# Block products for the first half of the tokens, a shared ring for weight chunks, early K rows and PSUM chains in a gated attention-MLP kernel

## The chip, the cores and the metric

The kernel runs on one core of a Trainium2 chip. The metric is the device time of one execution in microseconds (us). TensorE (PE, with its weight loads as PEld) multiplies; VectorE (DVE), ScalarE (ACT) and GpSimd (POOL) do the rest; SyncE (SP) issues most transfers. Each engine works through its own instructions strictly in the order in which the program gives them, and waits for others by semaphores.

## The reference

```python
x = A_x                                            # 1 x 2048 x 576, fp32
g = sigmoid((x * gate_w).sum(-1, keepdims=True))
a = A_ref(x, A_wqkv, A_wo)     # linear attention, 32 heads of 18, phi(t) = elu(t) + 1 + 1e-6
b = (gelu(x @ w_gate) * (x @ w_up)) @ w_down       # 576 -> 4608 -> 576
return g * a + (1 - g) * b
```

Everything is fp32. The kernel multiplies with TensorE's fp32r type and splits each operand into a high part (rounded to fp32r) and a low part (the rest): three matmuls, high by high, high by low and low by high, stand for one. Copying a tile into an fp32r tile on ScalarE makes the high part; one subtraction makes the low part.

## The kernel before, in words

Part one (to about 280 us) computes keys, values and queries, the attention state, and the gated attention result `g * a`, which goes to DRAM as `ga_d`, one piece for each of the 16 tiles of 128 tokens. The first loop over token tiles (`for t in range(2, NST)`) multiplies the keys and values; beside it, `Early` already prepares the weights of the first MLP chunk: it fetches them in pieces, forms four differences on GpSimd, the high part on ScalarE and the low part on GpSimd, and stores them to DRAM (`wp_d`).

Part two is the MLP. The tokens are taken in two pairs of 512-token blocks ("the first pair", "the second pair"), the 4608 hidden units in 18 chunks of 256 (`NF2`), so there are 36 chunks `n`, two loops of 18 in one. A chunk's gate and its up matrix are both computed as a 2 x 2 block product by seven products instead of eight (Strassen-Winograd): `product(k, m, ps, start)` issues seven matmuls of 128 x 512 for product k of matrix m (0 gate, 1 up) with operands `xo` (sums of token blocks, made ahead) and `W[m]` (sums of weight blocks). A step is one product and what follows on VectorE and ScalarE. Gate's steps end in a GELU into `es[0..3]`; up's steps multiply `es` by the up result and split the result into `hs[i]`, high and low.

The down projection of a chunk is issued during the next chunk, between the steps. For the first pair it is plain: `down(n, t)` is 12 matmuls of 128 x 288 for each of eight token tiles, and VectorE adds the result, times 1 − g, to an accumulator. For the second pair (all but its last chunk) it is by seven block products as well: `unit(n, k, q)` is six matmuls for half of product k, and VectorE adds the result to one of seven sums; three more operands (`hx`) and one in `hs` are sums of `es` blocks, made on GpSimd (`h_sums`). After the last chunk the seven sums are combined on GpSimd (`combine`), and the last chunk's plain down is added with the gates.

In the first pair the weights of each chunk are made as they are needed and stored for the second: SP fetches the raw block (`w_fetch`), GpSimd forms four differences (`w_sums`), ScalarE the high and GpSimd the low parts (`w_split`), SP stores the 2.2 MB tile to `wp_d`. In the second pair they are loaded from there (`w_load`). The sums of the second pair's tokens are also made during the first pair, in six pieces, each spread over two chunks (`sums_ahead`): fetched and summed in one, split and stored in the next.

PSUM has four single banks for the products (`bank()`) and two pairs of banks for the down projection (`pair()`). A new user of a buffer waits until the last reader of the old one is through. The order of the work is written out by hand: `next_down` puts units or down tiles between the steps, and each engine's queue follows the order of the program text.

Of the kernel before, what the change touches and what calls it, by code (L numbers as in the profile page):

```python
# [8 lines left out]
F32 = mybir.dt.float32  # L9
# [7 lines left out]
NB, BS = 4, 512  # L17
# [15 lines left out]
SEQUENCE = (1, 6, 2, 7, 5, 4, 3)  # L33
# [6 lines left out]
def tile_gated_mix(ctx, tc, xt, xs, wkv, wq, wo, wgu, wdn, cst, out):  # L40
# [134 lines left out]
    def kv_post(t, c, ps, part):  # L175
# [81 lines left out]

    class Early:


        def __init__(self, k):
            self.m, self.kt = divmod(k, 3)
            r, v = w_raw(), qw[k % 2].rearrange("p a c -> p (a c)")

            def part(a, c, n):
                return a[:, c * 128:(c + n) * 128].rearrange("p (i c) -> p i c", i=n)

            self.raw, self.sums, self.hi, self.lo = part(r, 0, 4), part(r, 4, 4), part(v, 0, 7), part(v, 7, 7)
            nc.sync.dma_start(self.raw, wgu[0, self.m, :, :, self.kt])

        def make(self):
            b12, b11, b21, b22 = (self.raw[:, i] for i in range(4))
            t1, t2, t3, t4 = (self.sums[:, i] for i in range(4))
            for o, a, b in ((t1, b12, b11), (t2, b22, t1), (t3, b22, b12), (t4, t2, b21)):
                nc.gpsimd.tensor_tensor(o, a, b, OP.subtract)
            for i, src in ((slice(0, 3), self.raw[:, 1:4]), (slice(3, 7), self.sums)):
                nc.scalar.activation(self.hi[:, i], src, AF.Copy)
                if self.kt < 2:
                    nc.gpsimd.tensor_tensor(self.lo[:, i], src, f32(self.hi[:, i]), OP.subtract)
                else:  # L280
                    nc.gpsimd.tensor_tensor(self.hi[64:96, i], src[64:96], f32(self.hi[64:96, i]), OP.subtract)

        def store(self):
            nc.sync.dma_start(wp_d[0][self.m][:, :, self.kt], f32(self.hi))
            if self.kt < 2:
                nc.sync.dma_start(wp_d[0][self.m][:, :, 3 + self.kt], f32(self.lo))

    early = []
    x_next(1)
    for t in range(2, NST):  # L290
# [26 lines left out]
    mixing.banks(3)  # L317
    denp = mixing.stack.enter_context(tc.tile_pool(name="denp", bufs=1, space=PSUM, reuse_waits="tile"))
# [197 lines left out]
    def mixed(b, t):  # L516
# [3 lines left out]
        for g in range(NG):  # L520
            R = GR[g]
            for a, wl in ((0, 0), (0, 1), (1, 0)):
                for i in range(2):
# [6 lines left out]
                             scale=gate[:, 0, st:st + 1])  # L530
# [564 lines left out]
```

## Time and profile before

| | us |
|---|---|
| median of 3 runs | 1556.26 (1552.9 to 1557.09) |
| span of the profiled execution | 1554.6 |
| PE busy | 1535.8 (99%) |
| DVE busy | 989.5 (64%) |
| POOL busy | 851.2 (55%) |
| ACT busy | 548.6 (35%) |
| gate and up products, PE (L690, two groups) | 433.7 + 435.8 |
| plain down, PE (L852, four groups) | 250.6 + 12.7 + 1.8 + 1.7 |
| units, PE (L876, two groups) | 123.0 + 93.0 |

The page gives no device time of its own for the profiled execution beside the span. In rows that group instructions, the columns are line, engine, operation, output <- inputs, shapes, count, then busy time in us, mean ns of one, and the idle time of the engine ahead of them with what ended it. In rows in order of time, they are start (us), length (us), engine, line, operation; the square bracket is the engine's idle time before the row and what ended it. Matmuls overlap their successors, so the distance between two starts, not the length, is what a matmul costs.

### The profile page before, as it was taken

The numbers are of one execution on the slowest core, as the hardware profiler recorded it, in microseconds if no ns is written. First come the engines' busy times: TensorE is split into PE (matmuls) and PEld (weight loads), VectorE is DVE, ScalarE is ACT, GpSimd is POOL, SyncE is SP. The second block draws the span as 40 slices with busy tenths as digits, with TensorE's granted clock in tenths as the row PEclk, the third lists the DMA queues.
The fourth block names the chain that finished last, engine by engine and source line by source line (L and its number), as shares of the span: only waits on it lengthen the run. The fifth ranks groups of instructions, "written<-read, shape, count | busy, mean of one in ns | idle before, by whom it ended". The sixth has DMA issues, their size and how long they took to land.

```text
span 1554.6 us, 21238 instructions
## 1 busy us (share of the span) xinstructions
PE 1535.8 (99%) x8447; PEld 1358.3 (87%) x8447; DVE 989.5 (64%) x1342; ACT 548.6 (35%) x848; POOL 851.2 (55%) x693
## 2 busy tenths in 40 slices
PE   8999999999999999999999999999999999999997
PEld 8999788888888888888888888888888888888886
DVE  6443767366655555565655556777777767777777
ACT  6544554333433333333333322223232223222221
POOL 1410112276777768686666646556666555666663
PEclk9999999999999999999999999999999999999999
DMA  5611434765556565565545575433443443344333
GB/s 202 194 56 32 154 126 170 254 254 188 204 203 235 218 230 202 188 242 186 215 177 194 202 312 184 180 142 134 175 167 134 148 179 134 141 186 150 134 149 107
DMA packets 53883, 275.26 MB, mean 177 GB/s; under 512 B 4368, under 2 KB 23464, under 8 KB 43160
## 3 DMA queue, kind: packets, MB, share of 16 engines
q1 hardware_dynamic: 49464, 257.26, 44.5%
q10 hardware_dynamic: 2592, 9.31, 1.6%
q0 software_dynamic: 1728, 7.34, 1.2%
q8 instruction: 66, 1.08, 0.3%
q14 instruction: 33, 0.27, 0.1%
HBM read 172.41 MB, written 101.47 MB: 176 GB/s over the span
## 4 chain that ended last, share of the span: by engine, by line
PE 91%; DVE 4%; DMA 2%; issue 1%; ACT 1%; POOL 1%; SPq 0%; ACTq 0%; DVEq 0%; POOLq 0%
PE bank L690 50%; PE pair L852 15%; PE pair L876 12%; PE bank L168 7%; PE bank L333 3%; PE pair L524 2%; PE pair L219 1%; DVE h L733 1%; DMA xc<-xs 1%; DMA wg<-wp_d 1%; POOL xo L476 1%; DVE e L727 0%; DVE sums L904 0%; PE pair L168 0%; PE den L428 0%
## 5 line engine op out<-in xcount | busy, mean ns | idle before, releaser
L690 PE MATMUL bank<-xo,wu 128*128 128x512 f32 x1764 | 435.8, 394 | 5.7 <-DVE p L790 5.7
L690 PE MATMUL bank<-xo,wg 128*128 128x512 f32 x1764 | 433.7, 393 | 0.2 <-DMA wg<-wp_d 0.2
L690 PEld LDWEIGHTS bank<-xo,wu 128*128 128x128 f32 x1764 | 323.4, 188 | 66.7 <-DVE p L790 6.6
L690 PEld LDWEIGHTS bank<-xo,wg 128*128 128x128 f32 x1764 | 324.8, 188 | 64.7 <-DMA wg<-wp_d 0.6
L852 PEld LDWEIGHTS pair<-wd,h 128*128 128x128 f32 x1716 | 243.6, 189 | 13.8 <-DVE wd L67 0.7
L852 PE MATMUL pair<-wd,h 128*128 128x288 f32 x1716 | 250.6, 294 | 0.7 <-DVE wd L67 0.5
L730 ACT ACTIVATE h<-e 128x512 fp32r<-128x512 f32 x127 | 80.4, 633 | 376.3 <-DVE e L727 349.6
L859 DVE SCALAR_TENSOR_TENSOR acc<-pair,gate,acc 128x576 f32<-128x576 f32 x143 | 116.6, 816 | 131.1 <-PE pair L852 131.1
L881 DVE TENSOR_TENSOR sums<-pair,sums 128x576 f32<-128x576 f32 x224 | 167.7, 754 | 34.3 <-PE pair L876 26.5
L733 DVE TENSOR_TENSOR h<-e,h 128x512 fp32r<-128x512 f32 x127 | 131.4, 1035 | 44.8 <-ACT h L730 44.7
L760 ACT ACTIVATE e<-e 128x512 f32<-128x512 f32 x108 | 68.1, 631 | 226.1 <-DVE e L816 93.4
L680 POOL TENSOR_TENSOR wdb<-draw,wdb 128x432 fp32r<-128x432 f32 x34 | 38.4, 1153 | 195.9 <-ACT wdb L678 195.9
L876 PEld LDWEIGHTS pair<-wdb,h 128*128 128x128 f32 x816 | 117.9, 189 | 8.3 <-DVE sums L881 0.6
L876 PE MATMUL pair<-wdb,h 128*128 128x288 f32 x816 | 123.0, 296 | 0.1
L168 PE MATMUL bank<-kvw,xo 128*128 128x378 f32 (+5 forms) x560 | 106.9, 345 | 5.4 <-ACT kvw L66 5.2
L168 PEld LDWEIGHTS bank<-kvw,xo 128*128 128x128 f32 (+1 forms) x560 | 97.0, 192 | 9.9 <-ACT kvw L66 5.6
L618 POOL TENSOR_TENSOR wu<-wuraw,wu 128x768 fp32r<-128x768 f32 x18 | 36.5, 2028 | 119.6 <-ACT wu L617 119.6
L876 PEld LDWEIGHTS pair<-wdb,hx 128*128 128x128 f32 x612 | 89.0, 189 | 6.2 <-DVE sums L881 0.6
L876 PE MATMUL pair<-wdb,hx 128*128 128x288 f32 x612 | 93.0, 296 | 0.1
L765 ACT ACTIVATE p<-bank 128x512 f32<-128x512 f32 x72 | 43.0, 598 | 122.0 <-PE bank L690 121.6
L770 DVE TENSOR_TENSOR u<-bank,p 128x512 f32<-128x512 f32 x72 | 49.4, 686 | 45.0 <-PE bank L690 39.9
L727 DVE TENSOR_TENSOR e<-u,e 128x512 f32<-128x512 f32 x72 | 69.4, 965 | 2.5
(171 smaller groups left out, 2079.2 us busy)
## 6 DMA issues: line engine op xcount, KB each, us to landing
wp_d<-wg SPq DMA_DIRECT2D x17, 2240.0 KB, 6.7
wp_d<-wu SPq DMA_DIRECT2D x17, 2240.0 KB, 8.2
wg<-wp_d SPq DMA_DIRECT2D x17, 2240.0 KB, 8.7
wu<-wp_d SPq DMA_DIRECT2D x17, 2240.0 KB, 8.4
draw<-wdn SPq DMA_DIRECT2D x36, 576.0 KB, 9.4
wgraw<-wgu SPq DMA_DIRECT2D x18, 768.0 KB, 4.4
wuraw<-wgu SPq DMA_DIRECT2D x18, 768.0 KB, 4.5
xo<-xop_d SPq DMA_DIRECT2D x7, 1280.0 KB, 8.1
```

Source lines behind the costliest of these rows:

```text
L168: nc.tensor.matmul(out_t[:, :n], xa, kvw[i][:rows, r, lo:lo + n], start=(k == 0), stop=(k == 13))
L333: nc.tensor.matmul(ps[:R], qw[i][:rows, rw, GO[g]:GO[g] + R], xa, start=(k == 0), stop=(k == 13))
L690: nc.tensor.matmul(ps, w_, x_, start=start and i == 0, stop=i == 6, skip_group_check=not start)
L727: nc.vector.tensor_tensor(es[i], v, es[i], OP.mult)
L730: nc.scalar.activation(hs[i][:, 0], es[i], AF.Copy)
L733: nc.vector.tensor_tensor(hs[i][:, 1], es[i], f32(hs[i][:, 0]), OP.subtract)
L760: nc.scalar.activation(es[i], es[i], AF.Gelu_apprx_tanh)
L770: nc.vector.tensor_tensor(u2, b, p1, OP.add)
L852: nc.tensor.matmul(y[i], h[:, a, c], wd[:, (1 - i, 2 + i)[f], wl], start=(k == 0), stop=(k == 5))
L859: nc.vector.scalar_tensor_tensor(o, v, gate[:, 1, st:st + 1], o, op0=OP.mult, op1=OP.add)
L876: nc.tensor.matmul(y[:, j, :288], h[:, hl, c], wd[:, b, wl], start=(i == 0), stop=(i == 2))
L881: nc.vector.tensor_tensor(o, y[:, :, :288], o, OP.add)
```

## The change

Four things are done. (1) The first pair's down projection also goes by units (17 of its 18 chunks), with the same `sums`, `hx` and `combine`; in the first pair the sums of h, their low parts and the low part of `wd` are made on VectorE, in the second on GpSimd. (2) Weight chunks come in halves through one ring of three tiles of 128 x 1152 (`Half`), shared by gate and up chunks, down chunks, the token pieces (now 12, each fetched and finished in one chunk) and the `ga_d` tiles. (3) The last 64 of the 576 K rows (`tail`, 32 rows in each half) of all chunks are prepared in the first loop over token tiles by `Early`, now 13 jobs instead of six, and come by six small transfers a chunk (`w_tail`). (4) Gate and up products are chained in PSUM: products 1, 6, 5, 3 accumulate in one bank and 7, 4 in another, and ScalarE copies what stands there after products 1, 6 and 5. The order of the products changes from 1, 6, 2, 7, 5, 4, 3 to 1, 7, 6, 2, 5, 3, 4.

Core of the diff (new lines, cut):

```diff
-SEQUENCE = (1, 6, 2, 7, 5, 4, 3)
+SEQUENCE = (1, 7, 6, 2, 5, 3, 4)
...
+    def block_sums(raw8, eng, c=slice(None)):
+        b12, b11, b21, b22, t1, t2, t3, t4 = (raw8[:, i, c] for i in range(8))
+        for o, a, b in ((t1, b12, b11), (t2, b22, t1), (t3, b22, b12), (t4, b21, t2)):
+            eng.tensor_tensor(o, a, b, OP.subtract)
...
+    JOBS = [("tail", 0)] + [("main", m, kt) for m in range(2) for kt in range(2)] + [("tail", i) for i in range(1, NF2 // 2)]
...
+        for _ in range(2):
+            if len(early) < len(JOBS):
+                early.append(Early(len(early), JOBS[len(early)]))
                 early[-1].make()
+                if len(early) > 1:
+                    early[-2].store()
...
+    def w_tail(n, m, queue=None):
+        q = slice((2 * m + n % 2) * 32, (2 * m + n % 2 + 1) * 32)
+        hi, lo = wt_d[n // 2]
+        for r, src in enumerate((hi, hi, lo)):
+            (queue or nc.sync).dma_start(f32(W[m][32 * r:32 * r + 32, :, 4]), src[q])
...
+    def d_split(parts, eng, plain=False):
+        for h in parts:
+            dst, src = (wd[:, :4], h.raw8[:, :4]) if plain else (wd, h.raw8[:, 1:])
+            nc.scalar.activation(dst[:, :, 0, h.c], src, AF.Copy)
+        for h in parts:
+            dst, src = (wd[:, :4], h.raw8[:, :4]) if plain else (wd, h.raw8[:, 1:])
+            eng.tensor_tensor(dst[:, :, 1, h.c], src, f32(dst[:, :, 0, h.c]), OP.subtract)
...
+    def w_make(h):
+        w = W[h.m]
+        block_sums(h.raw8, nc.gpsimd)
+        nc.scalar.activation(w[:, :, h.kt], h.raw8[:, 1:], AF.Copy)
+        nc.gpsimd.tensor_tensor(w[:, :, 2 + h.kt], h.raw8[:, 1:], f32(w[:, :, h.kt]), OP.subtract)
...
+    def x_make(h):
+        hi, lo = h.hi.bitcast(F32R), h.raw.bitcast(F32R)
+        sum_blocks(h.raw, nc.gpsimd)
+        nc.scalar.activation(hi, h.raw, AF.Copy)
+        if h.kt < 2:
+            nc.gpsimd.tensor_tensor(lo, h.raw, h.hi, OP.subtract)
+            nc.gpsimd.dma_start(xop_d[:, S2:S1 + 1, 3 + h.kt, h.c], h.raw)
...
+        nc.gpsimd.dma_start(xop_d[:, S2:S1 + 1, h.kt, h.c], h.hi)
...
+    def up_steps(plain, sum_eng, low_eng):
...
+        def s6():
+            product(6, 1, ps["a"], False)
+            nc.scalar.activation(u2, ps["a"], AF.Copy)
+        def s2():
+            c = bank()
+            product(2, 1, c, True)
+            nc.vector.tensor_tensor(c, c, p1, OP.add)
+            up(0, c)
+        def s5():
+            product(5, 1, ps["a"], False)
+            nc.scalar.activation(u3, ps["a"], AF.Copy)
+            high(hs[0], es[0])
+            nc.vector.tensor_tensor(u3, ps["b"], u3, OP.add)
+            up(3, u3)
+            low(hs[0], es[0])
+        def s3():
+            product(3, 1, ps["a"], False)
+            high(hs[3], es[3])
+            up(1, ps["a"])
+            high(hs[1], es[1])
+            low(hs[3], es[3])
+        def s4():
+            product(4, 1, ps["b"], False)
+            nc.vector.tensor_tensor(ps["b"], ps["b"], u2, OP.add)
+            up(2, ps["b"])
+            low(hs[1], es[1])
...
+            def first():
+                h_sum(3, 2, 3, OP.add)
+                h_sum(2, 0, 2, OP.subtract)
+                h_sum(0, 3, 0, OP.subtract)
+                h_sum(1, 1, 0, OP.subtract)
+                high(hb[S1], es[3])
+                high(hb[S3], es[2])
+            def second():
+                high(hb[S2], es[0])
+                high(hb[S4], es[1])
+                for a, i in ((S2, 0), (S3, 2), (S1, 3), (S4, 1)):
+                    low(hb[a], es[i], low_eng)
+            late.extend([first, second])
...
+        sum_eng, low_eng, d_eng = (nc.vector, nc.vector, nc.vector) if p == 0 else (nc.gpsimd, nc.gpsimd, nc.gpsimd)
...
+        gate_down = (0, 0, 0, 1, 1, 1, 1) if seam else (0, 0, 2, 3, 3, 2, 2) if final else (0, 0, 2, 2, 2, 2, 2)
+        for i, step in enumerate(gate_steps() if n else first_steps):
...
+            if late and i in (0, 1):
+                late.pop(0)()
+            next_down(gate_down[i])
+            if p == 0 and n:
+                if i == 0:
+                    w_tail(n, 1)
+                if i in (2, 3):
+                    w_make(ups.pop(0))
+                if i == 4:
+                    nc.sync.dma_start(wp_d[q][1], f32(W[1]))
+                    if 2 <= n < 14:
+                        xr_.append(x_fetch(n - 2))
+                if i == 5 and xr_:
+                    x_make(xr_.pop())
...
+            if i == 6:
+                if p == 0 and n + 1 < NF2:
+                    gates = w_fetch(n + 1, 0)
...
+        up_down = (0, 1, 1, 0, 2, 0, 0) if not final else (0, 0, 0, 0, 2, 0, 0)
+        for i, step in enumerate(up_steps(final, sum_eng, low_eng)):
             step()
+            next_down(up_down[i])
+            if p == 0 and n + 1 < NF2:
+                if i == 0:
+                    w_tail(n + 1, 0)
+                if i in (0, 1):
+                    w_make(gates[i])
+                if i == 2:
+                    ds = d_fetch(n)
+                    nc.sync.dma_start(wp_d[n + 1][0], f32(W[0]))
+                if i == 4:
+                    ups = w_fetch(n + 1, 1)
...
+            if not final and i == 3:
+                d_sums(ds)
+            if i == 5:
+                d_split(ds, d_eng, final)
```

`w_fetch`, `d_fetch` and `x_fetch` each take ring tiles and issue one SP transfer a tile (256 KB for weights and tokens, 288 KB for down). `combine` is called between the steps of the last chunk of both pairs.

What the engines' queues hold at three places. In the rows, `e`, `h` and `hx` are the tiles of `es`, `hs` and `hx`, and numbers tell tiles of one kind apart. First, VectorE at the turn from one chunk of the first pair to the next, before:

```order
L816 TENSOR_TENSOR u_2552<-bank,u_2552 128x512
L727 TENSOR_TENSOR e_2913<-u_2552,e_2913 128x512
L733 TENSOR_TENSOR h_2918<-e_2914,h_2918 128x512
L733 TENSOR_TENSOR h_2917<-e_2913,h_2917 128x512
L67 TENSOR_TENSOR wd<-draw,wd 128x4x288
L770 TENSOR_TENSOR u_2552<-bank,p_2551 128x512
L785 TENSOR_TENSOR u_2553<-bank,u_2552 128x512
L859 SCALAR_TENSOR_TENSOR acc_2927<-pair,gate,acc_2927 128x576
```

and now (L690 is wd's low part, L837, L799 and L751 belong to up's last product, L846 are the sums of h):

```order
L690 TENSOR_TENSOR wd<-ring,wd 128x7x144 x2
L837 TENSOR_TENSOR bank<-bank,u_2636 128x512
L799 TENSOR_TENSOR e_3001<-bank,e_3001 128x512
L751 TENSOR_TENSOR h_3004<-e_3000,h_3004 128x512
L846 TENSOR_TENSOR e_3002<-e_3001,e_3002 128x512
L846 TENSOR_TENSOR e_3001<-e_2638,e_3001 128x512
L846 TENSOR_TENSOR e_2638<-e_3002,e_2638 128x512
L846 TENSOR_TENSOR e_3000<-e_3000,e_2638 128x512
L751 TENSOR_TENSOR hx_3008<-e_2638,hx_3008 128x512
L751 TENSOR_TENSOR h_3005<-e_3001,h_3005 128x512
L751 TENSOR_TENSOR hx_3007<-e_3002,hx_3007 128x512
L751 TENSOR_TENSOR hx_3009<-e_3000,hx_3009 128x512
```

The first sums out of PSUM (L906) stand directly behind the last of these. Second, SP's queue in a chunk of the first pair, before (`xu` is the token piece):

```order
L660 DMA draw<-wdn 128x1152
L606 DMA wuraw<-wgu 128x1536
L622 DMA wp_d_1_108<-wu 128x4480
L700 DMA xu<-xs 128x4x256
L606 DMA wgraw<-wgu 128x1536
L622 DMA wp_d_0_109<-wg 128x4480
```

and now:

```order
L990 DMA wp_d_1_124<-wu 128x4480
L711 DMA ring<-xs 128x4x128
L697 DMA ring<-wgu 128x512 x2
L619 DMA wg<-wt_d_0_99 32x7x128 x2
L619 DMA wg<-wt_d_1_100 32x7x128
L674 DMA ring<-wdn 128x4x144 x2
L1023 DMA wp_d_0_125<-wg 128x4480
```

The gate chunks used to be fetched a chunk ahead, behind the token piece as now; they are now fetched for the next half of the work. Third, ScalarE around the start of the up products in the first pair, before (L705 splits a token piece, L617 the weights, L765 copies p1):

```order
L705 ACTIVATE xuh<-xu 128x1024
L776 ACTIVATE e_2554<-bank 128x512
L760 ACTIVATE e_2915<-e_2915 128x512
L760 ACTIVATE e_2914<-e_2914 128x512
L760 ACTIVATE e_2913<-e_2913 128x512
L765 ACTIVATE p_2551<-bank 128x512
L617 ACTIVATE wg<-wgraw 128x3x384
L617 ACTIVATE wg<-tsum 128x4x384
```

and now (L717 splits a token piece, L704 the weights, L804 and L812 copy p1 and u2 out of PSUM):

```order
L757 ACTIVATE e_2638<-e_2638 128x512
L757 ACTIVATE e_3002<-e_3002 128x512
L757 ACTIVATE e_3000<-bank 128x512
L717 ACTIVATE ring<-ring 128x512
L757 ACTIVATE e_3001<-e_3001 128x512
L804 ACTIVATE p_2635<-bank 128x512
L704 ACTIVATE wg<-ring 128x7x128 x2
L812 ACTIVATE u_2636<-bank 128x512
```

A copy that TensorE waits for now stands behind the two weight halves, and the token piece's split stands between the GELUs of the chunk that fetched it.

More of the change, by code (lines that the diff above doesn't have):

```diff
@@ L271, in make @@
-        def make(self):
[L272 to L281, printed above, removed]
@@ L283, in store @@
-        def store(self):
-            nc.sync.dma_start(wp_d[0][self.m][:, :, self.kt], f32(self.hi))
-            if self.kt < 2:
-                nc.sync.dma_start(wp_d[0][self.m][:, :, 3 + self.kt], f32(self.lo))
+            self.raw8 = r[:, :1024].rearrange("p (i c) -> p i c", i=8)
+            self.hi, self.lo = (v[:, a * 896:(a + 1) * 896].rearrange("p (i c) -> p i c", i=7) for a in range(2))
+            self.job = job
+            kind, *which = job
+            src = wgt[which[0]] if kind == "tail" else wgu[0, which[0], which[1]]
@@ L316, in tile_gated_mix @@
     mixing = Scope()
-    mixing.banks(3)
-    denp = mixing.stack.enter_context(tc.tile_pool(name="denp", bufs=1, space=PSUM, reuse_waits="tile"))
+    mixps = Scope()
+    mixps.banks(3)
+    denp = mixps.stack.enter_context(tc.tile_pool(name="denp", bufs=1, space=PSUM, reuse_waits="tile"))
     rp = mixing.pool("rp", bufs=3)
@@ L632, in tile_gated_mix @@
     scaled(0, 0)
-    nc.scalar.dma_start(f32(W[0]), wp_d[0][0])
+    first_load(0)
     mixed(3, 3)
@@ L676, in d_split, with __init__, as8 @@
-    def d_split():
-        for i, src in ((slice(0, 3), draw[:, 1:4]), (slice(3, 7), dsum)):
-            nc.scalar.activation(wd[:, i, 0], src, AF.Copy)
-            for c in (slice(0, 144), slice(144, 288)):
-                nc.gpsimd.tensor_tensor(wd[:, i, 1, c], src[:, :, c], f32(wd[:, i, 0, c]), OP.subtract)
+    class Half:
+        def __init__(self):
+            self.t = ring.tile([128, 1152], F32, name="ring")
+        def as8(self, c):
+            return self.t[:, :8 * c].rearrange("p (i c) -> p i c", i=8)
@@ new lines, in d_fetch, with d_sums @@
+    def d_fetch(n):
+        out = []
+        for c in range(2):
+            h = Half()
+            h.raw8, h.c = h.as8(144), slice(c * 144, (c + 1) * 144)
+            nc.sync.dma_start(h.raw8[:, :4], wdn[n % NF2][:, :, h.c])
+            out.append(h)
+        return out
+    def d_sums(parts):
+        for h in parts:
+            b12, b11, b21, b22, t1, t2, t3, t4 = (h.raw8[:, i] for i in range(8))
+            for o, a, b in ((t1, b12, b11), (t2, b22, t1), (t3, b22, b12), (t4, t2, b21)):
+                nc.gpsimd.tensor_tensor(o, a, b, OP.subtract)
@@ L841, in down, with acc_of @@
+        return [s1, s7, s6, s2, s5, s3, s4]
+    def acc_of(t):
+        return sums[:, 0:2, t] if t < 4 else sums[:, 2:4, t - 4]
+    def down(p, t):
+        single = p == NP - 1 and t == PER - 1
         if single:
@@ L913, in tile_gated_mix @@
     scaled(1, 0)
-    nc.scalar.dma_start(f32(W[1]), wp_d[0][1])
+    first_load(1)
     first_steps[3]()
@@ L920, in tile_gated_mix @@
     mixing.close()
-    mlp.banks(4)
+    nc.vector.tensor_scalar(gate, gate, -1.0, 1.0, op0=OP.mult, op1=OP.add)
     hp0 = mlp.pool("hp0")
@@ L1035, in tile_gated_mix @@
+    for t in range(8):
+        gated(1, t)
+        down(1, t)
     mlp.close()
```

434 lines of the change are left out of this document (160 added, 274 removed).

## The prediction

> **What bounds the kernel now.** I read the page's busy table first, then the engines stretch by stretch, then TensorE's rows in order of time.
>
> ```profile
> span 1554.6 us, 21238 instructions
> PE 1535.8 (99%) x8447; PEld 1358.3 (87%) x8447; DVE 989.5 (64%) x1342; ACT 548.6 (35%) x848; POOL 851.2 (55%) x693
> ```
>
> TensorE is busy for all but 19 us. The median of the runs shown, 1556.26, is 1.7 us above this span, and I make the sum against the span.
>
> ```profile
> core 0: us, PE busy (x) PEld busy (x) DVE busy (x) ACT busy (x) POOL busy (x), PEclk, DMA share, GB/s
> 385.27:420.60 35.33, 35.33 (x196) 31.16 (x194) 21.29 (x29) 12.97 (x16) 27.40 (x23) 1.00 0.63 246
> 991.22:1025.02 33.80, 33.80 (x183) 29.64 (x182) 24.79 (x31) 9.78 (x16) 19.96 (x17) 1.00 0.40 151
> ```
>
> These are one chunk of the first token pair (plain down) and one of the second (seven block products). In both TensorE never waits, at full clock, and 35.33 − 33.80 = 1.53 us is what the block products save on a chunk if TensorE goes on without waits.
>
> ```profile
> 994.45 1.75 PE L876 MATMUL pair<-wdb,h 128*128 128x288 f32 x12
> 996.04 1.78 PE L690 MATMUL bank<-xo,wg 128*128 128x512 f32 x7
> 997.67 1.75 PE L876 MATMUL pair<-wdb,hx 128*128 128x288 f32 x12
> ```
>
> From start to start: a gate or up product is 1.62 us, a unit 0.80. Fourteen of each make 33.9, the row's chunk. So what matters is whether ScalarE, VectorE, GpSimd and the transfers keep ahead of these steps in the new order. Their prices:
>
> ```profile
> L881 DVE TENSOR_TENSOR sums<-pair,sums 128x576 f32<-128x576 f32 x224 | 167.7, 754 | 34.3 <-PE pair L876 26.5
> L733 DVE TENSOR_TENSOR h<-e,h 128x512 fp32r<-128x512 f32 x127 | 131.4, 1035 | 44.8 <-ACT h L730 44.7
> L765 ACT ACTIVATE p<-bank 128x512 f32<-128x512 f32 x72 | 43.0, 598 | 122.0 <-PE bank L690 121.6 <-ACT ga L529 0.5
> L730 ACT ACTIVATE h<-e 128x512 fp32r<-128x512 f32 x127 | 80.4, 633 | 376.3 <-DVE e L727 349.6 <-PE bank L690 26.7
> L678 ACT ACTIVATE wdb<-draw 128x864 fp32r<-128x864 f32 x17 | 15.8, 928 | 29.7 <-PE pair L876 29.7
> L678 ACT ACTIVATE wdb<-dsum 128x1152 fp32r<-128x1152 f32 x17 | 19.6, 1151 | 2.8 <-POOL dsum L674 2.8
> L275 POOL TENSOR_TENSOR raw<-raw 128x128 f32<-128x128 f32 x24 | 11.7, 510 | 50.8 <-DVE e L188 24.4 <-DMA raw<-wgu 20.3 <-DVE xo L67 5.6
> L618 POOL TENSOR_TENSOR wg<-wgraw,wg 128x768 fp32r<-128x768 f32 x18 | 33.3, 1852 | 31.8 <-ACT wg L617 31.5
> L618 POOL TENSOR_TENSOR wu<-tsum,wu 128x1024 fp32r<-128x1024 f32 x18 | 43.2, 2401 | 1.4
> L741 POOL TENSOR_TENSOR hx<-e,hx 128x512 fp32r<-128x512 f32 x34 | 43.9, 1291 | 12.6 <-ACT hx L740 12.6
> L714 POOL DMA_DIRECT2D xop_d<-xuh x6 | 4.6, 762 | 0.6 <-POOL xuh L713 0.6
> ```
>
> and two VectorE instructions with no GpSimd work beside them:
>
> ```profile
> 390.30 1.36 DVE L67 TENSOR_TENSOR wd<-draw,wd 128x1152 fp32r<-128x1152 f32 x1 [0.36 <-ACT wd L66]
> 412.56 0.69 DVE L733 TENSOR_TENSOR h<-e,h 128x512 fp32r<-128x512 f32 x1 [0.70 <-ACT h L730]
> ```
>
> I use, by interpolation: VectorE 0.69 for 512 columns and 1.2 for a 1008-column low part; ScalarE 0.60 for a copy out of PSUM, 0.63 for a high part, 0.95 for 896 columns, 1.05 for 1008; GpSimd 2.16 for four weight sums, 2.13 for an 896-column low part, 2.36 for 1008.
>
> **The change part by part.**
>
> *Block products in the first pair.* 17 chunks go from 96 plain matmuls to 84: 17 × 1.53 = 26.0 us less TensorE work. Eight accumulator updates on VectorE give way to 14 unit sums, four sums of h, three more low parts of h, and two low parts of wd in place of one.
>
> *Products chained in PSUM.* Four VectorE additions a chunk go; four ScalarE copies come, and TensorE now waits for six copies: product 6 for p1, 5 for u2, 3 for u3. Between 5 and 3 stand two units (1.6 us) against 0.2 + 0.60, so by themselves they cost nothing. Their cover is ScalarE being free, which it is not, below.
>
> *VectorE at the end of a first-pair chunk.* I count from the end of up's product 3. VectorE first finishes what product 5 released (a copy, three operations, two unit sums): free 1.2 us later. Then `es[1]` 0.69, ScalarE's high part 0.63, ScalarE's first wd half 1.05, two L690 at 1.2, three operations 2.07, four sums of h and four low parts 5.52, and the first unit sum 0.75: 14.3 us in one row, because the order on VectorE puts L690 ahead of everything that product 4 releases. TensorE meanwhile has product 4, gate's 1, 7, 6, two units and product 2: 9.7 us. Its third unit needs the bank pair that the first unit sum frees, so it stands 4.6 us in every first-pair chunk. Even with no wait on ScalarE the VectorE work alone is 12.1 us plus the 0.25 until it starts: at least 2.6 us of stall, more than the 1.53 saved.
>
> *The loop through GpSimd, ScalarE and SP's queue.* Time 0 is the end of that first unit sum. The last sum of h ended at −3.5; ScalarE's high part, its copy of u2 and the high part of the first up chunk follow until −1.3; GpSimd's low part, the four sums of the second chunk, ScalarE, GpSimd: the up weights stand at 6.1. Only then does SP issue the 2.2 MB store of them, and behind it in the same queue the token piece and both gate chunks. What a transfer takes behind that store is shown by the kernel before, where the token piece is its successor too (SP's issues, and the first instruction that used it):
>
> ```profile
> 432.64 0.33 SPq L622 DMA_DIRECT2D wp_d<-wu  x1
> 433.02 0.59 SPq L700 DMA_DIRECT2D xu<-xs  x1
> 441.87 0.75 POOL L458 TENSOR_TENSOR xu<-xu 128x256 f32<-128x256 f32 x1 [5.11 <-DMA xu<-xs]
> raw<-wgu SPq DMA_DIRECT2D x6, 256.0 KB, 4.3
> ```
>
> 8.85 us for 512 KB behind the store; 4.3 for 256 KB behind stores of 448 KB, the lower bound. I take 8.85, since the place in the queue is the same. So the token piece lands at 15.35; GpSimd sums 2.16, ScalarE 0.63, GpSimd 1.29 and two issues of 0.77: 21.0. First gate chunk: sums 2.16, ScalarE 0.95, low part 2.13; second: sums 2.16, ScalarE 0.95: 29.35. ScalarE's copy of up's u2 is queued behind this last high part: 29.95. TensorE wants it for product 5 at 19.3 and stands until then, so product 3 ends at 29.95 + 1.62 + 1.6 + 1.62 = 34.8, and the next time 0 is 14.3 later: a chunk of 49.1 us. There are 12 chunks with a token piece. In the four others the gate chunks land at 15.35 instead: 24.3 for the copy, a chunk of 43.4. Against 35.33: 12 × 13.8 + 4 × 8.1 = +198 us. The bounds: with 4.3 for the landing −73; the low parts and sums at their mean beside GpSimd (1035 against 690 ns, some 12 on the path) +64.
>
> *Second pair.* Sums of h and their low parts stay on GpSimd, but wd's split moves one product later. From product 3's end: `es[1]` at 1.9, its high part 2.5, wd's halves on ScalarE 3.5 and 4.6, on GpSimd 5.9 and 8.25. The first unit, due at 6.5, needs both. GpSimd's sums end at 13.4, the low part that frees `es[0]` at 14.7; VectorE's new `es[0]` and the unit sums behind it, and ScalarE's copy of u2 (14.65) behind the high parts, let product 5 end at 16.3 instead of 12.9: 3.35 us × 17 = +57 us. Between 2.3 (ScalarE never waits) and 4.4 (a port wait on each chain) a chunk: +39 to +75.
>
> *K rows made early.* Thirteen jobs instead of six, two a token tile over tiles 2 to 8. What one costs ScalarE now, and TensorE's tile:
>
> ```profile
> 44.01 0.64 ACT L277 ACTIVATE qw<-raw 128x512 fp32r<-128x512 f32 x1 [1.76 <-POOL raw L275]
> 43.16 0.28 PE L219 MATMUL pair<-vt,pkh 128*126 128x254 f32 x1
> 51.67 0.28 PE L219 MATMUL pair<-vt,pkh 128*126 128x254 f32 x1
> ```
>
> A tile takes 8.5 us. Two jobs in a row hold ScalarE for 0.95 + 2.13 + 2.16 + 0.95 = 6.2, beside about 5.2 of its own work: up to 12 a tile, six times: 0 to +24, I take +15 since four PSUM banks cover some of it. In the main loop it removes GpSimd's third-row instructions (two to four of 1.0 to 1.4 us a weight) and adds six small transfers a chunk on SP, which wait only for weights long done: nothing.
>
> *Edges.* A first 4.6 us stall, chunk 0 (no units between its products), and the turn to plain down at the end of the pair: about +10 (0 to 15). At the very end the 14 combining sums now stand apart. Before, in a row:
>
> ```profile
> 1507.98 19.48 POOL L890 TENSOR_TENSOR sums<-sums 128x576 f32<-128x576 f32 x14
> 1523.59 7.13 DVE L733 TENSOR_TENSOR h<-e,h 128x512 fp32r<-128x512 f32 x1 [0.70 <-ACT h L730]
> 1532.17 3.35 PE L690 MATMUL bank<-xo,wu 128*128 128x512 f32 x7 [5.18 <-DVE p L790]
> ```
>
> That 5.2 us stall I let go: −5 (−5 to +5).
>
> The sum: 1554.6 + 198 + 57 + 15 + 10 − 5 = 1830 us (rounded terms; 1829 unrounded).
>
> **The shared port, weighed.** In the last rows a VectorE instruction of 0.69 took 7.13 while GpSimd ran 14 instructions back to back at 1.39 each. The Trainium skill (SBUF — State Buffer, Who interferes with whom) says that a VectorE instruction with two SBUF inputs and a GpSimd instruction exclude each other for their whole length. The trace agrees by that row. As a mechanism of this kernel it would hold a first-pair chunk with a token piece to GpSimd's 4 × 4.29 + 8 × 0.54 (144 columns, from the 128-column row) + 3.45 = 24.9 plus VectorE's 12 × 0.69 + 2 × 1.2 = 10.7: 35.6 us, and no less.
>
> **The rivals.**
>
> *The loop is hidden, the VectorE row alone decides.* If the store is drained quickly (4.3 landing), chunks are 44.5 and 38.9; if all of GpSimd's work is in time, 19.3 + 4.84 + 14.3 = 38.5. Times 1683 to 1757. For it: 256 KB is half of 512. Against: the same place in the queue.
>
> *It does what it says.* TensorE runs at 33.9 in both pairs: 1554.6 − 26.0 = 1528.6. It decides if VectorE's row after product 3 fits in 9.7 us and the copy of u2 is there at 19.3. For it: VectorE is busy only 24.79 of 33.80 in the second pair. Against: the 12.1 us of VectorE work in that place.
>
> *The port alone binds.* 12 chunks of 35.6, the rest at 33.9: +3 − 7, about 1551, no change. Against: it hides every in-order wait.
>
> **How the numbers follow.** Loop 0.66 (1770 to 1890 by its terms), VectorE row alone 0.20, gain 0.07, no change 0.04, a small loss (1560 to 1680) 0.03. About 0.3% is what a measurement of this kernel can tell from no change. Slower 0.89, same 0.04, faster 0.07. The range 1690 to 1890 holds the loop and most of the VectorE case, some 8 in 10; the likeliest case's own is 1770 to 1890.
>
> **What would show it.** First-pair chunks near 49 and 43 us instead of 35.33; TensorE idle twice in each, before the third unit with VectorE's unit sum as releaser, and before up's product 5 with ScalarE's copy; GpSimd waiting for the token piece some 9 us after the store; second-pair chunks near 37; VectorE still below 90% busy. It is wrong if TensorE has no idle time ahead of those two places, or if the token piece lands within 5 us.

## The result, and the profile after

The changed kernel takes 1880.67 us (median of 4 runs, 1879.1 to 1883.37) against 1556.19 for the kernel before: a ratio of 1.209, interval 1.207 to 1.211. It is 324 us slower. The forecast was 1829, range 1690 to 1890. All line numbers in this part are those of the changed kernel (there L733 is a product's matmul, L901 a unit's), except where another kernel is named.

The busy table of the profiled execution; TensorE's share has fallen from 99 to 87%, VectorE's from 64 to 54, GpSimd's from 55 to 46; no engine has taken TensorE's place:

```profile
span 1877.3 us, 21720 instructions
PE 1632.5 (87%) x8243; PEld 1411.5 (75%) x8243; DVE 1018.2 (54%) x1444; ACT 648.9 (35%) x1065; POOL 872.9 (46%) x994
```

TensorE is also busy for longer (1632.5 instead of 1535.8 us) with 204 fewer matmuls. The stretches show where. Rows are the 12 chunks with a token piece, three without, and 16 of the second pair (columns: window, its length, then busy time of PE, PEld, DVE, ACT, POOL; then the granted clock of TensorE, the DMA share and GB/s):

```profile
394.13:994.04 599.91, 469.63 (x2186) 398.40 (x2184) 321.13 (x446) 191.67 (x289) 311.28 (x416) 0.88 0.47 153
994.04:1124.75 130.71, 111.40 (x547) 95.36 (x546) 79.08 (x111) 46.02 (x69) 64.22 (x84) 0.92 0.49 158
1211.42:1812.58 601.16, 566.72 (x2914) 488.03 (x2912) 329.90 (x432) 190.19 (x303) 303.04 (x288) 0.97 0.38 139
```

That is 50.0, 43.6 and 37.6 us a chunk (forecast 49.1, 43.4, 37.15), against 35.33 and 33.80 in the kernel before. By the starts of the gate products the 322.7 us between the two spans are: up to the first gate product +22.6; chunk 0 +13.5; chunk 1 +8.1; chunks 2 to 13 +175.9; 14 to 16 +24.7; 17 and 18 together +14.2; 19 to 34 +60.1; the end +3.5.

One such chunk in TensorE's order. The two waits are where the forecast put them, ahead of the third unit and of up's product 5:

```profile
506.83 3.25 PE L901 MATMUL pair<-wd,h 128*128 128x288 f32 x12 [3.17 <-DVE sums L906]
509.88 3.02 PE L733 MATMUL bank<-xo,wg 128*128 128x512 f32 x7
528.26 1.78 PE L733 MATMUL bank<-xo,wu 128*128 128x512 f32 x7
536.10 3.36 PE L733 MATMUL bank<-xo,wu 128*128 128x512 f32 x7 [6.06 <-ACT u L812]
539.26 2.07 PE L901 MATMUL pair<-wd,hx 128*128 128x288 f32 x12
```

Behind each wait stands something that I had not forecast: seven matmuls take 3.16 us from start to start (536.10 to 539.26) instead of 1.62. The granted clock is 0.50 there, and also behind the first wait, where hardly any transfer runs (DMA share 0.02); it is back at 1.00 a little later, under heavy transfers (1.03). In the columns of the stretches:

```profile
506.83:509.88 3.05, 3.05 (x12) 3.05 (x13) 1.97 (x3) 0.00 (x0) 2.94 (x5) 0.50 0.02 5
536.10:539.26 3.16, 3.16 (x7) 2.48 (x8) 0.00 (x0) 0.00 (x0) 3.08 (x5) 0.50 0.22 91
541.20:544.40 3.20, 3.20 (x16) 2.61 (x16) 3.20 (x5) 0.63 (x1) 0.84 (x1) 1.00 1.03 358
```

The loop that makes the second wait, in the rows of SP, GpSimd and ScalarE:

```profile
513.03 0.33 SPq L990 DMA_DIRECT2D wp_d<-wu  x1
513.47 0.58 SPq L711 DMA_DIRECT2D ring<-xs  x1
521.94 0.46 POOL L466 TENSOR_TENSOR ring<-ring 128x128 f32<-128x128 f32 x1 [8.94 <-DMA ring<-xs]
534.62 0.95 ACT L704 ACTIVATE wg<-ring 128x896 fp32r<-128x896 f32 x1 [3.94 <-POOL ring L264]
535.47 0.58 ACT L812 ACTIVATE u<-bank 128x512 f32<-128x512 f32 x1
```

Store, token piece behind it, its first use 8.47 us later (taken: 8.85), the gate weights, and only then the copy of u2 for which TensorE waits.

### The profile page after: what moved, and what is told of

It is laid out like the page before. It is cut to its first block, busy times and chain, and to the rows that moved or that the text cites. A ratio compares the mean times of both kernels' runs of the same rounds, so it can differ in the third digit from the quotient of the medians.

```text
span 1877.3 us, 21720 instructions
## 1 busy us (share of the span) xinstructions
PE 1632.5 (87%) x8243; PEld 1411.5 (75%) x8243; DVE 1018.2 (54%) x1444; ACT 648.9 (35%) x1065; POOL 872.9 (46%) x994
## 3 DMA queue, kind: packets, MB, share of 16 engines
q8 instruction: 65, 1.06, 0.2%
## 4 chain that ended last, share of the span: by engine, by line
PE 37%; POOL 19%; DVE 14%; DMA 13%; issue 9%; ACT 7%; SPq 1%; ACTq 0%; POOLq 0%; DVEq 0%
PE bank L733 18%; PE pair L901 10%; DMA ring<-xs 5%; POOL wd L690 5%; DMA ring<-wgu 4%; POOL ring L264 3%; PE bank L170 3%; DVE e L799 2%; DVE sums L906 2%; PE bank L342 2%; POOL wg L705 2%; DVE e L846 2%; ACT wd L687 2%; POOL e L846 2%; DVE h L751 1%
## 5 line engine op out<-in xcount | busy, mean ns | idle before, releaser
L733 PE MATMUL bank<-xo,wu 128*128 128x512 f32 x1764 | 465.9, 415 | 109.8 <-ACT u L812 84.2
L906 DVE TENSOR_TENSOR sums<-pair,sums 128x576 f32<-128x576 f32 x448 | 329.6, 753 | 302.5 <-PE pair L901 296.4
L733 PEld LDWEIGHTS bank<-xo,wu 128*128 128x128 f32 x1764 | 342.0, 200 | 189.6 <-ACT u L812 91.6
L733 PE MATMUL bank<-xo,wg 128*128 128x512 f32 x1764 | 464.1, 411 | 8.6 <-ACT u L770 7.8
L733 PEld LDWEIGHTS bank<-xo,wg 128*128 128x128 f32 x1764 | 342.6, 200 | 84.2 <-ACT u L770 11.5
L901 PE MATMUL pair<-wd,h 128*128 128x288 f32 x1632 | 269.9, 317 | 89.8 <-DVE sums L906 58.4
L901 PEld LDWEIGHTS pair<-wd,h 128*128 128x128 f32 x1632 | 251.9, 205 | 113.0 <-DVE sums L906 65.5
L690 POOL TENSOR_TENSOR wd<-ring,wd 128x1008 fp32r<-128x1008 f32 (+1 forms) x36 | 90.1, 2524 | 304.5 <-ACT wd L687 304.5
L264 POOL TENSOR_TENSOR ring<-ring 128x128 f32<-128x128 f32 x272 | 149.6, 570 | 139.7 <-DMA ring<-wgu 134.0
L901 PEld LDWEIGHTS pair<-wd,hx 128*128 128x128 f32 x1224 | 192.8, 204 | 16.6 <-issue 1.8
L901 PE MATMUL pair<-wd,hx 128*128 128x288 f32 x1224 | 197.6, 309 | 2.6 <-DVE sums L906 2.6
L682 POOL TENSOR_TENSOR ring<-ring 128x144 f32<-128x144 f32 x272 | 135.6, 524 | 38.4 <-issue 33.1
L705 POOL TENSOR_TENSOR wu<-ring,wu 128x896 fp32r<-128x896 f32 x34 | 76.1, 2240 | 120.4 <-ACT wu L704 120.4
L751 DVE TENSOR_TENSOR h<-e,h 128x512 fp32r<-128x512 f32 x127 | 128.6, 1014 | 0.1
L748 ACT ACTIVATE hx<-e 128x512 fp32r<-128x512 f32 x102 | 64.4, 632 | 177.5 <-POOL e L846 110.5
L705 POOL TENSOR_TENSOR wg<-ring,wg 128x896 fp32r<-128x896 f32 x34 | 71.0, 2090 | 44.9 <-ACT wg L704 43.8
L846 POOL TENSOR_TENSOR e<-e,e 128x512 f32<-128x512 f32 x68 | 87.4, 1285 | 4.0
```

The costliest lines, as they stand in the source:

```text
L264: eng.tensor_tensor(o, a, b, OP.subtract)
L690: eng.tensor_tensor(dst[:, :, 1, h.c], src, f32(dst[:, :, 0, h.c]), OP.subtract)
L705: nc.gpsimd.tensor_tensor(w[:, :, 2 + h.kt], h.raw8[:, 1:], f32(w[:, :, h.kt]), OP.subtract)
L733: nc.tensor.matmul(ps, w_, x_, start=start and i == 0, stop=i == 6, skip_group_check=not start)
L748: nc.scalar.activation(dst[:, 0], src, AF.Copy)
L751: (eng or nc.vector).tensor_tensor(dst[:, 1], src, f32(dst[:, 0]), OP.subtract)
```

## The experiments

**The loop of the first pair.** Two runs move fetches in SP's queue.

```diff
                 if i == 4:
-                    nc.sync.dma_start(wp_d[q][1], f32(W[1]))
                     if 2 <= n < 14:
                         xr_.append(x_fetch(n - 2))
+                    gates = w_fetch(n + 1, 0)      # second run only; taken out at i == 6
+                    nc.sync.dma_start(wp_d[q][1], f32(W[1]))
```

> SP issues the token piece's fetch ahead of the 2.2 MB store of the up weights instead of behind it; nothing else moves. Loop (landing behind the store is on the path): the piece is at hand when GpSimd has the up weights done, its work is over before the gate chunks land, and a chunk with a token piece becomes like one without, 43.6 instead of 50.0 us: 12 x -6.4 = -77, some 1804 us. VectorE row alone: no chunk changes, 1881. If what lengthens a token chunk is GpSimd's own 5.7 us for the piece and not where it lands: also no change, 1881.

> SP issues the token piece and both gate chunks ahead of the store. Loop: from the end of the first unit sum GpSimd now has up weights to 6.1, token piece to 11.8, first gate chunk to 16.1, second gate chunk's high part at 19.2, the copy of u2 at 19.8 against the 19.3 at which product 5 wants it: the second stall goes and the VectorE row alone is left, 38.5 us a chunk in all 16 chunks: 12 x -11.5 + 4 x -5.1 = -158, some 1722 us (1710 to 1750). VectorE row alone as the whole cause: no change, 1881. If the store's traffic only meets the fetches elsewhere (they slow one another): chunks of 42 to 44, some 1780 to 1800.

1795.47 and 1756.77 us (ratios to the kernel before 1.153 and 1.128). Chunks with a token piece, of the first run and of the second:

```profile
393.21:911.27 518.06, 446.94 (x2186) 381.43 (x2184) 321.11 (x446) 192.69 (x289) 310.05 (x416) 0.92 0.52 177
```

```profile
390.97:882.84 491.87, 436.03 (x2186) 370.23 (x2184) 319.87 (x445) 190.95 (x288) 305.05 (x416) 0.95 0.54 187
```

50.0 falls to 43.2 by the order of two instructions: a token chunk is now as long as one without. With the gate chunks ahead too it is 41.0, in chunks with and without a piece. So the landing behind the store is on the path; the two rivals by which e1 would change nothing are ruled out. But 41.0 is not the 38.5 of the VectorE row. TensorE in the second run:

```profile
608.55 2.30 PE L901 MATMUL pair<-wd,h 128*128 128x288 f32 x12 [3.99 <-DVE sums L906]
610.65 2.95 PE L733 MATMUL bank<-xo,wg 128*128 128x512 f32 x7
630.25 1.89 PE L733 MATMUL bank<-xo,wu 128*128 128x512 f32 x7 [0.55 <-ACT u L812]
```

The second wait is down to 0.55, the first stays with 3.99, and slow matmuls follow it. Next I took away what the row holds.

```diff
-                for a, i in ((S2, 0), (S3, 2), (S1, 3), (S4, 1)):
-                    low(hb[a], es[i], low_eng)
+                # VectorE: S2 and S1 behind the units of gate step 2, S3 behind those of 3, S4 of 4
-            if i == 5:                             # second run: 4, in both pairs
                 d_split(ds, d_eng, final)
```

> The fetches ahead of the store (as in the run before of that name), and in the first pair the four low parts of the sums of h are issued on VectorE behind the first unit sums instead of ahead of them. VectorE row (what is left of the 40.98 us is the wait of 4.0 before the third unit, the half pace of TensorE after it, some 2.4, and 0.6 before product 5): the row is shorter by 4 x 0.69 = 2.76, the wait 1.2, too short for half pace: chunk 33.9 + 1.2 + 0.6 = 35.7, 16 x -5.3 = -85, some 1672 us. GpSimd and VectorE share a port and their sum binds: at least 35.6 with a token piece, about 34 without. Rival (the wait only moves to the later low parts or to ScalarE): 39 to 41 a chunk, no more than -30.

> As e5_lows_later, and wd's split one product earlier in both pairs. VectorE row: two low parts of wd (2 x 1.2) and ScalarE's two halves leave it, no wait before the third unit: 33.9 to 34.5 a chunk; with -3.0 in each of 16 second-pair chunks some 1672 - 24 - 47 = 1600 us. Port alone: 35.6 in the 12 chunks with a token piece, 33.9 in the others: some 1615 us. Rival (GpSimd's sums of wd come later than the split wants them, ScalarE waits, and the copies behind it): first-pair chunks stay at 36 or grow.

1758.34 us: nothing gained, a miss. 1682.93 us: chunks of 39.8 and 39.0, a miss in the first pair as well; of the 75 us gained on e5_lows_later most are the second pair's, whose chunks fall from 37.6 to 34.6. In e5_lows_later (TensorE, GpSimd, ScalarE):

```profile
603.41 1.88 PE L905 MATMUL pair<-wd,h 128*128 128x288 f32 x12 [1.52 <-DVE sums L910]
610.95 2.86 PE L733 MATMUL bank<-xo,wg 128*128 128x512 f32 x7 [2.46 <-ACT u L779]
604.75 2.45 POOL L705 TENSOR_TENSOR wu<-ring,wu 128x896 fp32r<-128x896 f32 x1 [5.40 <-ACT wu L704]
```

The wait for VectorE fell to 1.52 (1.2 reckoned), and the rest came back 5 us later as a wait for ScalarE's copy of gate's u3. ScalarE stood before the second up chunk, whose sums GpSimd had queued behind the first one's low part, which waited for ScalarE. The next run breaks this knot, and also fetches the first up chunk ahead of the store of the gate weights (the lines are shortened):

```diff
-                if i in (2, 3):  w_make(ups.pop(0))        # sums, high, low
+                if i == 2:       w_sums(ups)               # both chunks' sums; gates alike
+                if i in (2, 3):  w_make(ups.pop(0))        # high, low
```

> As e6_lows_split, and on GpSimd the sums of both chunks of a weight stand ahead of the first one's low part, and the first up chunk is fetched ahead of the 2.2 MB store of the gate weights. In e6 the second up chunk's sums stood behind a low part that waited for ScalarE, ScalarE for them, and TensorE 2.42 us for ScalarE's copy of gate's u3, with half pace after it. Theory (GpSimd and ScalarE waiting for each other in turn): first-pair chunks 39.8 and 39.0 to 34 to 35, 16 x -5 = -80, some 1603 us. Port alone: 35.6 with a token piece, 33.9 without: some 1607; what tells the two apart is whether the chunks with a piece are 1.7 us longer than those without and whether TensorE still waits. Rival (GpSimd, 26 us of work a chunk, is late with the sums of wd, which ScalarE now waits for ahead of its other work): 37 or more.

1624.54 us. Its token chunks, and those without:

```profile
385.06:818.37 433.31, 414.81 (x2185) 356.10 (x2184) 321.98 (x445) 194.02 (x288) 332.77 (x415) 0.99 0.60 211
818.37:923.74 105.37, 103.21 (x547) 88.45 (x546) 79.62 (x112) 46.25 (x70) 69.34 (x86) 1.00 0.57 201
```

36.1 and 35.1 a chunk, short of the 34 to 35 expected (1603 us); TensorE's clock is all but full, and it is busy for 34.4 us in a chunk without a piece. Of the 14.7 us by which a token chunk was too long, 13.9 are now shown to be order: SP's queue (9.0 with what hangs on it), VectorE's and ScalarE's rows (1.2), the knot and that fetch (3.7, changed together and not told apart).

Four of the twelve token chunks take 36.5 to 38.2, the others 35.1 to 35.8. In these four TensorE waits 1.74 to 2.60 us for ScalarE's copy of gate's p1, and ScalarE had stood before wd's halves, waiting for GpSimd's sums. One of them:

```profile
636.65 1.05 ACT L687 ACTIVATE wd<-ring 128x1008 fp32r<-128x1008 f32 x1 [2.32 <-POOL ring L682]
639.55 1.05 ACT L687 ACTIVATE wd<-ring 128x1008 fp32r<-128x1008 f32 x1 [1.85 <-POOL ring L682]
643.78 3.25 PE L736 MATMUL bank<-xo,wg 128*128 128x512 f32 x7 [2.60 <-ACT p L765]
```

So the rival of this run, GpSimd late with the sums of wd, holds in these four. In the short chunks the same wait for p1 is 0.3 to 1.1 us.

**The second pair.** In e3_split_earlier wd's split stands one product earlier, there alone.

> Second pair alone: wd's split one product earlier (behind product 5 instead of product 3), as in the kernel before. Theory (the order on ScalarE and GpSimd behind product 3 makes both waits): chunk 37.57 to about 34, 16 x -3.6 = -57, some 1823 us, and the first pair stays at 50.0 and 43.6. Rival (GpSimd's sum of work or the ring of three buffers binds the second pair): 37 or more, at most -10 us.

1826.18 us; the first pair is unchanged, and 16 chunks of the second take 34.7 each:

```profile
1209.44:1764.19 554.75, 545.76 (x2914) 474.73 (x2912) 319.62 (x433) 192.23 (x304) 312.22 (x289) 1.00 0.41 150
```

The place of the split was 2.9 of the 3.8 us, not all.

**Half pace.** In the 12 token chunks TensorE is busy for 469.63 us; twelve times 34.4 are 413. So 57 us, 4.7 a chunk, are matmuls at a lower pace. The trace's record of the granted clock agrees: 117 us of that busy time are at 0.50, which costs half of it. Does the wait cause it, or what runs beside? I gave TensorE more to do:

```diff
+            if i == 3 and 2 <= n < 14:             # gate: once, ahead of the third unit
+                product(2, 0, ups_ps["c"], True)
+            if i == 3 and 2 <= n < 14:             # up: three times, ahead of product 5
+                product(2, 1, gps["c"], True)
```

> The changed kernel with more work: in the 12 chunks with a token piece TensorE repeats product 2 once ahead of the third unit and three times ahead of up's product 5, into a PSUM bank that nothing reads, 28 matmuls or 6.5 us a chunk inside the two waits. Theory (after a wait of 3 us and more the next product runs at half pace, 3.16 instead of 1.62 us, and product 5 and a little behind it lie on the loop): with the waits cut below 3 us TensorE stays at full pace, and chunks fall from 50.0 to about 48: 12 x -1.8 = -22, some 1859 us, although work is added. Rival (the slow products come from the transfers or the other engines' traffic at that time, not from the wait): products stay slow, the repeats cost what the waits don't cover: 0 to +40 us, 1881 to 1920.

1871.8 us, ratio 1.200 to 1.204 against 1.207 to 1.211: with 6.5 us of added matmuls in each of 12 chunks the kernel is 9 us faster.

```profile
528.35 6.72 PE L733 MATMUL bank<-xo,wu 128*128 128x512 f32 x28
536.34 1.89 PE L733 MATMUL bank<-xo,wu 128*128 128x512 f32 x7 [1.27 <-ACT u L810]
538.07 1.78 PE L899 MATMUL pair<-wd,hx 128*128 128x288 f32 x12
604.06 3.25 PE L899 MATMUL pair<-wd,h 128*128 128x288 f32 x12 [2.35 <-DVE sums L904]
```

At the same place product 5 takes 1.73 us (536.34 to 538.07) behind a wait of 1.27 instead of 3.16 behind 6.06. From product 5 to the next chunk 6.57 us pass instead of 8.29. It is the wait: transfers don't explain it, since the slow units at 506.83 have a DMA share of 0.02 and the full pace from 541.20 has 1.03 (rows above). The gain is 9 and not 22 us because in some chunks the repeats outlast the wait (the twelve take 47.8 to 52.0), and because 2.35 us behind a repeat still bring two slow units (last row).

The Trainium skill (TensorE: Matmul & The Clock Gate, Part 1) says that TensorE's clock falls to half after an idle window of about 3.4 us and comes back after about as long busy, the window running free. The factor agrees (3.16 / 1.62 = 1.95), and so does the window: in the trace the half clock comes in stretches of 3.41 us or whole multiples, nearly all of them. The length of wait that it takes does not agree. In the changed kernel all 25 waits of 3.4 us and more from 394 us on are followed by half clock, but so are eleven of the fifteen waits of 1.70 to 1.72 us in the second pair, with no other wait of over 0.3 us in the 29 us ahead of them (the last row is a stretch):

```profile
1443.34 2.15 PE L901 MATMUL pair<-wd,h 128*128 128x288 f32 x11 [1.71 <-POOL wd L690]
1445.29 2.96 PE L733 MATMUL bank<-xo,wg 128*128 128x512 f32 x7
1445.00:1447.00 2.00, 2.00 (x8) 1.61 (x7) 0.83 (x2) 0.83 (x2) 1.92 (x2) 0.50 0.38 115
```

Waits of 2.35 and 2.46 us did it in the runs above (604.06 and 610.95). What decides in between, the place in a free-running window or how busy TensorE was in it, isn't shown.

**Plain products instead of block products.** Once with all else as in the changed kernel, once with all mended that is told here.

```diff
-            downs = deque((lambda u=u: unit(q == 1, *u)) for u in ...)     # p == 0 only
+            downs = deque((lambda t=t: down_plain(t, q == 1)) for t in range(8))
-        up_steps(final, sum_eng, low_eng)
+        up_steps(final or p == 0, sum_eng, low_eng)
```

> First pair with plain down products again (96 matmuls a chunk, no sums of h, no combining sums for this pair); shared ring, early rows and the chain in PSUM stay. Loop: ScalarE has no high part of an h sum ahead of the first up chunk, so the up weights stand about 15.5 us behind the end of product 3 instead of 20.4; store, landing and gate weights as before: copy of u2 at 39.4, chunk about 43 with a token piece and 37 without: 12 x -7 + 4 x -6.6 = -110, some 1770 us. VectorE row alone: with its sums and low parts gone the chunk falls to TensorE's own 35.33: 12 x -14.7 + 4 x -8.3 = -210, some 1670 us.

> e10_all with the first pair's down projection by plain products again (no sums of h there and no combining sums for this pair): what the block products are worth once ring, splits and edges are mended. Theory (they take 1.53 us of TensorE work from a chunk, and what VectorE and GpSimd pay for them comes back as waits): plain chunks run at TensorE's own 35.33 against 36.3 with a token piece and 35.1 without in e10: 12 x -0.9 + 3 x +0.2, -10 us, and some -5 at the turn of the pairs where the combining sums go: some 1585 us (1580 to 1600). Rival (the ring itself keeps the first pair above 35.33 in either form): no change, 1600 or more.

1823.55 us, with 47.0 and 38.3 a chunk: the plain chunk stays far above 35.33, so the block products are not the main cause: with what stays (ring, store, early rows, the chain in PSUM) a token chunk is still 11.7 us too long. The 43 was too low: no unit lies between products 5, 3 and 4, and all three run slow.

```profile
666.48 3.36 PE L733 MATMUL bank<-xo,wu 128*128 128x512 f32 x7 [5.30 <-ACT u L812]
670.58 5.77 PE L733 MATMUL bank<-xo,wu 128*128 128x512 f32 x14 [0.75 <-ACT u L822]
```

e12_all_plain: 1608.67 us (ratio 1.032 to 1.035), slower than e10_all (below) with block products, 1600.09 (1.026 to 1.029). Its plain chunks take 37.0, not 35.33. There the 0.75 us for ScalarE's copy of u3 stands in every chunk too: the chain in PSUM, which I costed at nothing because two units lie between products 5 and 3, costs where none do. My expectation that the plain form would gain some 15 us was wrong: as built here it loses about 1.0 us a chunk (37.0 against 36.0 on average). How much of that is the products themselves isn't shown, since the 0.75 us hang on where the plain tiles stand.

**Key-value stage and edges.** Two runs: the jobs spread over the tile, fetched a tile ahead, with first stores and one load earlier (e7_rows_edges); then all of it together, the jobs' low parts on VectorE.

> The changed kernel with two other places mended, the loop left alone. Key-value stage: four buffers instead of two, a pair of jobs fetched one token tile ahead, and each job's sums, copy and low part issued behind the tile's three projections in turn instead of all at its end. Edges: the first gate and up weights are stored as soon as they are loaded, and the second pair's first up weights are loaded ahead of the first rows of the output. Theory (ScalarE stands behind fetch and sums of each job; the first store holds back the gate weights; SP holds back one load): stage +21 to about +5, chunk 0 56.9 to about 46, the turn of the pairs -5: some 1850 us, first-pair chunks unchanged at 50.0 and 43.6. Rival (GpSimd's 8.6 us a tile against TensorE's 8.56 binds the stage): stage still +15 or more, some 1862 us.

> All that the runs so far point to: e9_sums_ahead with the edges of e7_rows_edges, and the key-value stage's jobs spread over the tile with their low parts on VectorE instead of GpSimd (in e7 GpSimd had 5.4 us a job, two jobs a tile of 8.56). Theory: e9 less 8 for the edges and 15 to 18 for the stage (tiles back to 9 us or less): some 1578 us. If VectorE has no room in the stage: -8 to -10 only, 1594 us. Below the kernel before (1556) it comes only if the first pair's chunks are under 34 us.

1871.2 us instead of 1850: 1.4 from the stage, 4.7 from chunk 0 (56.9 to 52.1; 46 expected), 3.3 from the turn of the pairs. Then 1600.09 us: 24 less than e9_sums_ahead, as reckoned, 16 of them in the stage; the total is 22 above the 1578 expected because e9 itself came out 22 above its 1603. The stretch of 80 us in the stage, of the changed kernel, of e7 and of e10:

```profile
40.00:120.00 80.00, 67.25 (x370) 63.59 (x369) 31.42 (x67) 39.85 (x88) 50.52 (x56) 0.94 0.68 222
```

```profile
40.00:120.00 80.00, 66.89 (x368) 62.80 (x367) 34.42 (x68) 37.56 (x82) 46.79 (x55) 0.91 0.63 217
66.50 2.09 POOL L283 TENSOR_TENSOR qw<-raw,qw 128x896 fp32r<-128x896 f32 x1 [1.06 <-ACT qw L282]
```

```profile
40.00:120.00 80.00, 77.38 (x462) 74.53 (x461) 46.80 (x88) 43.09 (x97) 25.74 (x36) 0.98 0.64 217
```

GpSimd bound the stage, as the rival said: 2.27 us of sums, 1.06 of waiting for ScalarE (the row of e7), 2.1 for the low part, 5.4 a job and two jobs a tile of 8.56. With the low parts on VectorE TensorE is back at 77.38 of 80. e10_all is the best form of the changed kernel here, and 2.7% slower than the kernel before. The 45 us left are the stage 8, chunk 0 5.5, chunks 2 to 16 some 10, the turn 9, the second pair 13.

**The end of the kernel before.** The price that I had put on its last rows was worth a run by itself: `combine` there with `slice(0, 1152)` instead of two slices of 576.

> The kernel before, with the combining sums at its end as 7 instructions of 1152 columns instead of 14 of 576. Port theory (GpSimd's instructions back to back, each on columns that the one just before doesn't write, shut VectorE out for 7.13 us): now each depends on the one just before, VectorE gets in between, the 5.18 us stall of TensorE shrinks: -2 to -5 us, 1552 to 1554. Rival (VectorE is shut out for the whole length of each, now twice as long): no change or up to +3.

1553.62 us against 1556.4, 0.9981 (0.9972 to 0.9991): 2.8 us (0.2%) faster than the kernel before, and the one version that beats both. Its rows:

```profile
1508.09 19.32 POOL L890 TENSOR_TENSOR sums<-sums 128x1152 f32<-128x1152 f32 x7
1523.67 1.21 DVE L733 TENSOR_TENSOR h<-e,h 128x512 fp32r<-128x512 f32 x1 [0.70 <-ACT h L730]
1531.18 0.85 PE L852 MATMUL pair<-wdb,h 128*128 128x288 f32 x2 [1.96 <-POOL wdb L668]
```

The same 19.3 us on GpSimd; VectorE's low part takes 1.21 instead of 7.13; TensorE's wait of 5.18 is gone, and 1.96 for GpSimd takes part of its place. In the kernel before, the 7.13 us (1523.59 to 1530.72) outlast the 14 sums, which end at 1527.46: two low parts of wd follow on GpSimd until 1530.18 without a gap, and VectorE is through 0.54 us behind the last.

In e8 not every sum depends on the one before, as the expectation has it, but four of the last six. Ahead of these four GpSimd is idle for 0.08 us, ahead of the other two not at all, and the low part ends 0.55 us behind the start of the last such gap (1524.33). So VectorE got in at a gap. That isn't the whole reading: the VectorE instruction that starts at 1526.31 ends at 1527.97, 0.56 us behind the end of the last sum, at a border with no gap. Why it gets in there, and not at such borders in the kernel before, stays open.

## Why the prediction was right, and where it was short

- **The loop** was right in place and length: 49.1 against 50.0 and 43.4 against 43.6, both waits with their releasers, landing 8.5 for 8.85. e1 and e2 show that SP's queue is on the path. The waits themselves are shorter than forecast, 3.17 for 4.6 and 6.06 for 10.65 (29.95 − 19.3): TensorE is at half pace behind the first one and so spends part of the loop's time working slowly instead of waiting.
- **Half pace was missed.** "product 3 ends at 29.95 + 1.62 + 1.6 + 1.62" took full pace for granted behind a wait; the slow product 5 and what follows add 1.7 (8.29 − 6.57). That the chunk came out only 0.9 above is in part luck: other steps were a little high. In the chunk shown the copy of u2 ends 29.3 us behind time 0 (506.78) for 29.95, and from product 3's end to the next time 0 VectorE's row takes 13.8 for 14.3. The row was there: in the prediction's quoted row at 1532.17 seven matmuls take 3.35 us behind a wait of 5.18.
- **VectorE row alone** is ruled out as the whole (e1, e2). As a share it was too simple: e5 shortened the row and a second chain, GpSimd and ScalarE in turn, took its place within the same 41 us.
- **It does what it says** is ruled out by the waits. **The port alone**: with the waits mended (e9) eight of the twelve chunks with a piece take 35.1 to 35.8, those without 35.0 to 35.4, so no extra 1.7 us for the piece is seen; a floor near 35 for both isn't ruled out. Nor was the price of the six small transfers a chunk, put at nothing, tried by a run of its own.
- **Second pair**: 37.6 for 37.15, and e3 shows the cause for 2.9 of the 3.8. Here too TensorE waits less than the 3.35 forecast: 2.15 us a chunk, and the rest is mostly slow pace (busy 566.72 us instead of e3's 545.76, with as many matmuls). That costs nothing there: chunks with a slow stretch and chunks without take the same 37.6.
- **Mis-sized terms.** Edges +10 − 5: measured chunk 0 +13.5, the turn +14.2, the end +3.5. Chunk 0 waits 7.65 us, since the first gate weights can't be written until their store, which is issued at 324.82, is done:

```profile
340.65 3.35 PE L733 MATMUL bank<-xo,wu 128*128 128x512 f32 x7 [7.65 <-ACT u L812]
334.27 0.95 ACT L704 ACTIVATE wg<-ring 128x896 fp32r<-128x896 f32 x1 [5.47 <-DMA wp_d<-wg]
```

  The key-value stage: +22.6 up to the first gate product for +15. I counted ScalarE; the bound was GpSimd (e7, e10). Of the 48 us by which the span exceeds 1829 the edges make 23 (31 against 5, where 3 of the second pair's forecast belong to a chunk within the edges), the first pair's chunks 11, the stage 8, the second pair's other 16 chunks 6.

## What to carry to other kernels

When a buffer is shared, write down for each queue what is issued ahead of what: a large store of a result is best issued behind the fetches that the next step needs, and the sums of two tiles ahead of the first one's dependent half, if another engine answers in between. Removing one wait of an in-order loop tells only what the next chain allows (e5); go on until TensorE's busy time alone is left. And price a long TensorE wait (here always from 3.4 us, at times from 1.7) at the wait and the slow matmuls behind it, and look for it in a profile as busy time that grew with no more matmuls.

## What the hardware showed

Matmuls at half clock behind waits, 57 us more busy time in the changed kernel's 12 token chunks, behind waits as short as 1.7 us elsewhere, and a kernel that gets faster by added matmuls. And VectorE's instruction of 0.69 us takes 7.13 beside a gapless row of GpSimd instructions, none of which needs the result of the one before, and 1.21 beside 7 larger ones, four of which do, though these sums fill the same 19.3 us.
